# A spectral filter block on one core: the 2-D transform factored over the 128 row blocks first, then the columns, then one matrix per frequency group

## The chip, the core and the metric

The kernel runs on one core of one Trainium2 chip. The core has a matrix engine (TensorE, called PE in the profile; PEld is its weight load), a vector engine (DVE), a scalar engine (ACT), a general engine (POOL) and a synchronising engine (SP) that issues nearly all DMA transfers. The engines run their own instruction lists in order and meet at semaphores. PE writes only to PSUM, a small accumulation memory of eight banks; DVE and ACT copy results from there to SBUF. The metric is the device time of one execution in microseconds (us); lower is better.

## The reference, cut to what matters

```python
mod = (silu(c) @ w_mod)                   # -> sa, ca, ga, sb, cb, gb, each 640 wide
h = layernorm(x) * (1 + ca) + sa          # x: 2048 rows, 640 columns, bf16
X = rfft2(h, axes=(rows, columns))        # 2048 x 321 complex
y = irfft2(X * (w_r + 1j * w_i))          # the learned filter, 2048 x 321
x = x + ga * y
h = layernorm(x) * (1 + cb) + sb
x = x + gb * ((silu(h @ w_gate) * (h @ w_up)) @ w_down)     # 1728 hidden
```

## The kernel before

Row s of x is written s = 16p + t, with p = 0..127 on the partitions and t = 0..15 as 16 tiles of 128 rows by 640 columns. A row frequency k is written with 128 values k1 and 16 values k2. Column frequencies l and 320 - l are handled together: sums and differences of even and odd columns give both.

**Forward stage** (functions `ln1_*`, `turn`, `turned`, `dfwd`, `zcopy`, `s1`, `acopy`, in an order written out by hand in the string `plan`). For each tile t, DVE takes the statistics (L280, L283), ACT the square root (L251), DVE the reciprocal and the normalised tile `xn` (L293). PE turns it in five 128x128 transposes (L301), the turned tile is copied out, and six products of 328 columns against the table `Rs` (the column transform, with 1 + ca folded in) make `zps` (L309). After a copy (L318) eight products against `Gtab` (L332, L333) do the 128-point transform over p with the twiddle factors of t; the copy L343 stores `A_sb`.

**Middle stage** (`transposed`, `t2`, `stage_a`, `product`, `stage_b`, `evict_y`, `stage_c`). For 41 groups of four column frequencies, and their mirrored partners, blocks of `A_sb` are transposed, 64 of them by eight DMA transposes (L434), the rest on PE (L446). Two products with a 128x128 table do the 16-point transform over t (L463, L464), ACT copies `X` (L466), POOL adds the transform of sa in one row (L469), DVE multiplies by the filter (L479, two instructions for each `X`), PE turns back and adds the two halves of the complex product by multiplying with the identity (L488), the result is copied (L496, L498) and multiplied back over t (L512, L513) into `Ep` (L517, L519). The filter lies in `Wb` and in `Wq`, which is the mirrored half; `Wq` comes through a DRAM copy `Wneg` that reorders it (L217 to L223). One of its copies has its sign turned on DVE (L360).

**Inverse stage** (`s1inv`, `dinv`). For each t, ten products of 128 columns transform back over p (L673 to L679), ACT copies `VT` (L681, L682), six products of 320 columns transform back over d (L689), and DVE adds the result to x in two instructions (L692). The statistics of the second layer norm for the first four tiles are taken in between (L621 to L623), and `Rinv_sb` holds the inverse column table times ga.

**Feed-forward stage**: four blocks of 512 rows, each with 27 groups of five products of 512 columns (L727, L740), a Silu on ACT (L743), a product on DVE (L744), then 8 x 14 products of 320 columns (L774) and a store (L777).

SP issues transfers in program order, and the framework gives SP's transfers eight semaphores in turn, so that a transfer waits for the eighth one before it. PE, DVE, ACT and POOL also keep program order. PSUM tiles are shared by tag; a tag with one or two buffers makes the writer wait for the copy of an earlier tile.

Of the kernel before, what the change touches and what calls it, by code (L numbers as in the profile page):

```python
# [18 lines left out]
LH = 164  # L19
L = 2 * LH  # L20
NG = 41
LP = 2 * NG
LW = 324
# [12 lines left out]


_TABLE_CACHE = {}


def _tables():
# [3 lines left out]
    l = np.arange(161, dtype=np.float64)[None, :]  # L45
# [8 lines left out]
    p = np.arange(P, dtype=np.float64)[:, None]  # L54
    k1 = np.arange(128, dtype=np.float64)[None, :]
    G = np.zeros((P, NT, 3, 128))
    for t in range(NT):
        a = 2.0 * np.pi * ((k1 * (16 * p + t)) % S) / S
        G[:, t, 0, :] = np.cos(a)
        G[:, t, 1, :] = -np.sin(a)  # L60
        G[:, t, 2, :] = np.sin(a)
    T["G"] = G.astype(_NPBF)
    kk = np.arange(128, dtype=np.float64)[:, None]
    pp = np.arange(P, dtype=np.float64)[None, :]
    H = np.zeros((128, NT, 3, P))
    for t in range(NT):
        a = 2.0 * np.pi * ((kk * (16 * pp + t)) % S) / S
        H[:, t, 0, :] = np.cos(a)
        H[:, t, 1, :] = np.sin(a)
        H[:, t, 2, :] = -np.sin(a)  # L70
    T["H"] = H.astype(_NPBF)

    F16 = np.exp(-2j * np.pi * np.outer(np.arange(16), np.arange(16)) / 16)

    def fwd(F, turn):
        M = np.zeros((16, 2, 4, 2, 16, 4))
        for j in range(4):
            i = 3 - j if turn else j
            M[:, 0, j, 0, :, i] = F.real
            M[:, 1, j, 0, :, i] = -F.imag  # L80
            M[:, 0, j, 1, :, i] = F.imag
            M[:, 1, j, 1, :, i] = F.real
        return M.reshape(128, 128)


    def inv(F, turn):
        M = np.zeros((2, 16, 4, 16, 2, 4))
        for j in range(4):
            i = 3 - j if turn else j
            M[0, :, i, :, 0, j] = F.real  # L90
            M[1, :, i, :, 0, j] = -F.imag
            M[0, :, i, :, 1, j] = F.imag
            M[1, :, i, :, 1, j] = F.real
        return M.reshape(128, NT, 2, 4)

    G16 = np.exp(+2j * np.pi * np.outer(np.arange(16), np.arange(16)) / 16)
    K = np.zeros((128, 9, 128))
    K[:, 0, :] = fwd(F16, False)
    K[:, 1, :] = fwd(F16[:, ::-1], True)
    K[:, 2, :] = -K[:, 1, :]  # L100
    a, b = inv(G16, False), inv(G16[::-1], True).reshape(128, 128)
    K[:, 3, :] = K[:, 4, :] = a.reshape(128, 128)
    K[:, 5, :], K[:, 6, :] = b, -b

    K[:, 7, :] = np.stack([-a[:, :, 1], a[:, :, 0]], axis=2).reshape(128, 128)
    K[:, 8, :] = a.reshape(128, 128)
    T["K"] = K.astype(_NPBF)
# [4 lines left out]
    for odd in range(2):  # L112
        dd = 2 * h + odd

        def re_row(ll):
            return (1.0 if ll == 0 else 2.0) * np.cos(2.0 * np.pi * ((dd * ll) % D) / D) / (S * D)

        def im_row(ll):
            if ll == 160:
                w = -np.sin(0.5 * np.pi * dd) if odd else np.cos(0.5 * np.pi * dd)  # L120
                return 2.0 * w / (S * D)
            return -2.0 * np.sin(2.0 * np.pi * ((dd * ll) % D) / D) / (S * D)

        for r in range(128):
            Rinv[r, odd, 0] = re_row(r)
            Rinv[r, odd, 1] = im_row(r + 1)
        for r in range(32):
            Rinv[64 * odd + r, odd, 2] = re_row(128 + r)
            Rinv[64 * odd + 32 + r, odd, 2] = im_row(129 + r)
# [6 lines left out]
def adaln_block_kernel(  # L136
# [15 lines left out]
    G_dram = nc.inline_tensor(T["G"], name="tab_G").ap()  # L152
    H_dram = nc.inline_tensor(T["H"], name="tab_H").ap()
    K_dram = nc.inline_tensor(T["K"], name="tab_K").ap()
# [11 lines left out]
    Ktab = const.tile([P, 9, 128], BF16, name="Ktab")  # L166
# [3 lines left out]
    shat = const.tile([1, 2, 2, LH], F32, name="shat")  # L170
# [8 lines left out]
    identb = const.tile([P, 128], BF16, name="identb")  # L179
    sc_f = const.tile([P, NC5], F32, name="sc_f")  # L180
    sc_col = const.tile([P, NC5], BF16, name="sc_col")
    sa_col = const.tile([P, NC5], BF16, name="sa_col")
    sEO = const.tile([1, 2, 2, LH], F32, name="sEO")

    x_sb = big.tile([P, NT, D], BF16, name="x_sb", tag="b20")
    wm_ca = big.tile([P, NC5, D], BF16, name="wm_ca", tag="epx")
    wm_sa = big.tile([P, NC5, D], BF16, name="wm_sa", tag="b21b")
    wm_g = big.tile([P, NC5, 2 * D], BF16, name="wm_g", tag="wg")
    wm_sb = big.tile([P, NC5, D], BF16, name="wm_sb", tag="wu")
    Rinv_sb = big.tile([P, 2, 3, 320], BF16, name="Rinv_sb", tag="ri")  # L190
    Rp = big.tile([P, 6, L], BF16, name="Rp", tag="rp")
    Rs = big.tile([P, 6, L], BF16, name="Rs", tag="rs")
    Gtab = big.tile([P, NT, 3, 128], BF16, name="Gtab", tag="gt")
    Wb = big.tile([P, 3, NT, LH], BF16, name="Wb", tag="wb")
    Wq = big.tile([P, 3, NT, 160], BF16, name="Wq", tag="b35")
    Htab = big.tile([P, NT, 3, 128], BF16, name="Htab", tag="ht")

# [24 lines left out]
    for i in range(2):  # L222
        nc.sync.dma_start(Wq[:, i], Wneg[i])  # L223
# [47 lines left out]
    with tc.tile_pool(name="ph1", bufs=3) as ph1, \  # L271
# [39 lines left out]
        def dfwd(t):  # L311
            zs[t] = ps1.tile([P, 2, 512], F32, name="zps")
            for r in range(2):
                dmm(zs[t][:, r, :L], t, r)
# [511 lines left out]
```

## Time and profile before

| what | us |
|---|---|
| median of 3 runs | 280.5 (280.18 to 281.39) |
| the profiled execution, its own time | 280.83 |
| its span in the profile | 279.0 |
| forward stage, to the first transposing DMA | 0 to 37.7 |
| middle stage | 37.7 to 74.0 |
| inverse stage | 74.0 to 97.6 |
| feed-forward stage | 97.6 to 279.0 |

The span is what the instructions cover; 1.8 us of the execution lie outside it. A group line of the profile gives a kind of instruction, how many there were, their busy time and the mean duration of one. Instructions of one engine overlap a little, so a row of equal ones starts at shorter distances than a duration: five products of 128x512 last 379 ns each in the groups and take 1.08 us together.

### The profile page before, as it was taken

The page shows a single profiled execution, that of the slowest core. Times are in us where ns is not written, and L with a number is a line of the kernel's source. Part 1 is how long each engine was busy: PE and PEld are TensorE (multiplying, and loading weights), DVE is VectorE, ACT ScalarE, POOL GpSimd, SP SyncE. Part 2 cuts the span into 40 slices and gives each one's busy share as a digit, 9 for nine tenths or more (in the row PEclk, how much of TensorE's full clock was granted, in tenths as well). Part 3 has the DMA queues.
Part 4 walks back from the last instruction along what each step waited for, and adds up shares of the span by engine and source line. Part 5 has one row for each costly group of instructions (what it writes and reads, how often), then busy time and mean ns, then how long its engine had stood idle before and what let it go on. Part 6 is the DMA issues. An engine that isn't in the chain of part 4 may idle for free.

```text
span 279.0 us, 5262 instructions
## 1 busy us (share of the span) xinstructions
PE 268.6 (96%) x2120; PEld 170.3 (61%) x2120; DVE 163.6 (59%) x411; ACT 112.8 (40%) x220; POOL 10.5 (4%) x34
## 2 busy tenths in 40 slices
PE   6899979999899999999999999999999999999995
PEld 6567768998787844446754445764444774444673
DVE  4999966799499738876227845224872422422322
ACT  5998666998455663222022323003233103223000
POOL 1000023312000010000000000000000000000000
PEclk9999999999999999999999999999999999999999
DMA  7989999999994100050110050101013011000011
GB/s 263 411 220 209 349 324 183 220 307 366 356 363 77 29 27 6 0 96 0 49 56 3 0 96 0 47 26 33 0 33 63 25 47 35 1 0 2 0 47 47
DMA packets 40634, 30.82 MB, mean 110 GB/s; under 512 B 29281, under 2 KB 37410, under 8 KB 40482
## 3 DMA queue, kind: packets, MB, share of 16 engines
q1 hardware_dynamic: 40608, 30.49, 38.3%
q8 instruction: 16, 0.26, 0.4%
q14 instruction: 8, 0.07, 0.1%
q10 hardware_dynamic: 2, 0.00, 0.0%
HBM read 22.88 MB, written 3.93 MB: 96 GB/s over the span
## 4 chain that ended last, share of the span: by engine, by line
PE 74%; DMA 10%; SPq 9%; DVE 4%; ACT 1%; issue 1%; ACTq 0%; DVEq 0%
PE gps L740 20%; PE ups L740 20%; PE ob L774 11%; PE oa L774 10%; DMA Wd_sb<-in_B_w_down_dram 4%; SPq L218 4%; DMA wm_sa<-in_w_mod_dram 3%; DMA Gtab<-tab_G 2%; PE oa L689 2%; SPq L596 2%; PE gu L727 2%; PE ob L689 1%; DVE x_sb L692 1%; SPq L223 1%; PE yps L488 1%; PE xps L463 1%
## 5 line engine op out<-in xcount | busy, mean ns | idle before, releaser
L740 PE MATMUL gps<-h2T_all,Wg 128*128 128x512 bf16 x260 | 64.6, 379 | 0.0
L740 PE MATMUL ups<-h2T_all,Wu 128*128 128x512 bf16 x260 | 64.6, 379 | 0.0
L743 ACT ACTIVATE sg<-gps 128x512 f32<-128x512 f32 x52 | 31.0, 597 | 74.0 <-PE gps L740 72.3
L740 PEld LDWEIGHTS <-Wu 128*128 128x128 bf16 x260 | 25.5, 98 | 30.6
L740 PEld LDWEIGHTS <-Wg 128*128 128x128 bf16 x260 | 25.4, 98 | 30.5
L744 DVE TENSOR_TENSOR ATb<-ups,sg 128x512 bf16<-128x512 f32 x26 | 17.9, 690 | 32.0 <-PE ups L740 32.0
L744 DVE TENSOR_TENSOR ATa<-ups,sg 128x512 bf16<-128x512 f32 x26 | 17.9, 687 | 20.4 <-PE ups L740 17.5
L774 PEld LDWEIGHTS <-ATa 128*128 128x128 bf16 x224 | 21.9, 98 | 9.3 <-issue 0.5
L774 PEld LDWEIGHTS <-ATb 128*128 128x128 bf16 x224 | 21.9, 98 | 8.8
L730 ACT ACTIVATE sg<-gu 64x512 f32<-64x512 f32 x4 | 2.3, 586 | 46.6 <-PE gu L727 46.6
L776 DVE TENSOR_TENSOR xo<-ob,x_sb 128x320 bf16<-128x320 f32 x16 | 7.9, 492 | 22.1 <-PE ob L774 22.1
L776 DVE TENSOR_TENSOR xo<-oa,x_sb 128x320 bf16<-128x320 f32 x16 | 7.8, 491 | 18.4 <-PE oa L774 18.4
L774 PE MATMUL oa<-Wd_sb,ATa 128*128 128x320 bf16 x112 | 16.8, 299 | 0.1
L774 PE MATMUL oa<-Wd_sb,ATb 128*128 128x320 bf16 x112 | 16.5, 299 | 0.0
L774 PE MATMUL ob<-Wd_sb,ATb 128*128 128x320 bf16 x112 | 16.5, 299 | 0.0
L774 PE MATMUL ob<-Wd_sb,ATa 128*128 128x320 bf16 x112 | 16.5, 299 | 0.0
L309 PE MATMUL zps<-Rs,hT 128*128 128x328 bf16 x90 | 14.7, 303 | 0.1
L280 DVE BATCH_NORM_STATS2 st<-x_sb 128x6 f32<-128x320 bf16 x32 | 13.8, 470 | 0.8 <-DMA x_sb<-in_A_x_dram 0.8
L681 ACT CAST VT<-va 128x512 bf16<-128x512 f32 x16 | 9.4, 586 | 8.0 <-PE va L677 6.2
L488 PE MATMUL yps<-identb,PP 128*128 128x128 bf16 x162 | 11.5, 219 | 0.6 <-DVE PP L479 0.4
L466 ACT CAST X<-xps 128x512 bf16<-128x512 f32 (+1 forms) x21 | 11.2, 598 | 1.6 <-PE xps L464 1.6
L309 PEld LDWEIGHTS <-hT 128*128 128x128 bf16 x96 | 8.8, 98 | 4.8 <-ACT hT L305 0.8
(204 smaller groups left out, 407.0 us busy)
## 6 DMA issues: line engine op xcount, KB each, us to landing
out_dram<-xo SPq DMA_DIRECT2D x16, 160.0 KB, 1.8
Wg<-in_B_w_gate_dram SPq DMA_DIRECT2D x1, 2080.0 KB, 12.8
Wd_sb<-in_B_w_down_dram SPq DMA_DIRECT2D x1, 2080.0 KB, 13.4
Wu<-in_B_w_up_dram SPq DMA_DIRECT2D x1, 2080.0 KB, 9.7
x_sb<-in_A_x_dram SPq DMA_DIRECT2D x3, 640.0 KB, 9.3
wm_g<-in_w_mod_dram SPq DMA_DIRECT2D x2, 800.0 KB
Gtab<-tab_G SPq DMA_DIRECT2D x4, 384.0 KB, 8.2
Htab<-tab_H SPq DMA_DIRECT2D x1, 1536.0 KB, 7.1
```

The source lines that it names most:

```text
L218: nc.sync.dma_start(to[0:15, 0], wv[1:16, 0])
L280: nc.vector.bn_stats(sts[t][:, h, :], x_sb[:, t, 320 * h:320 * h + 320])
L309: nc.tensor.matmul(zap, lhsT=hTs[t][:, 2 * r + i, :], rhs=Rs[:, 3 * r + i, :], start=(i == 0), stop=(i == 2))
L466: nc.scalar.copy(X[:, :n].rearrange("p i c k j -> p i (c k j)"), xps[:, :n, :])
L488: nc.tensor.matmul(yps[:, i, :], lhsT=PP[:, i, cp].rearrange("p a k j -> p (a k j)"), rhs=identb[:], start=(cp == 0), stop=(cp == 1))
L681: nc.scalar.copy(VTs[t][:, 0:4, :], va[:])
L689: nc.tensor.matmul(os_[odd][:], lhsT=VT[:, 2 * odd + ci if ci < 2 else 4, :], rhs=Rinv_sb[:, odd, ci, :], start=(ci == 0), stop=(ci == 2))
L740: nc.tensor.matmul(o[:], lhsT=w_[:, c5, fc * 128:(fc + 1) * 128], rhs=h2T[:, :, c5, :], start=(c5 == 0), stop=(c5 == NC5 - 1))
L743: nc.scalar.activation(sg[:], gps[:], ACT.Silu)
L744: nc.vector.tensor_tensor(AT[:, fc, :], ups[:], sg[:], ALU.mult)
L774: nc.tensor.matmul(os_[h][:], lhsT=AT[:, fc, tok], rhs=Wd_sb[:, fc, h * 320:(h + 1) * 320], start=(fc == 0), stop=(fc == NFC - 1))
L776: nc.vector.tensor_tensor(xo[:, h * 320:(h + 1) * 320], os_[h][:], x1[:, t, h * 320:(h + 1) * 320], ALU.add)
```

## The change

The same function is computed with the three partial transforms in another order.

- **Over p first, without turning x.** A tile's five blocks of 128 columns are the stationary operand, and a real 128x128 table `Fs` (cosines and sines of the 128-point transform, times the row's 1/std) is the moving one, so one product transforms over p and turns at once (`turn`). The mean is taken off by four products with the negated mean, in a high and a low bf16 part made on POOL (`means`). There is no normalised tile and no twiddle table `Gtab`.
- **Then over d**, for 16 groups g of 8 rows of that result times 16 t: six products of 324 columns (`dfwd`), as before.
- **Then over t with a matrix for each group** (`over_t`), which holds the 16-point transform, the twiddles and the recombination of the real transform, and makes l and 320 - l side by side. The filter is multiplied on (`product`), the complex sums and the sums of the two halves are made on DVE (`sums`), and `over_t_back` multiplies by the group's inverse matrix.
- **Back over d, then over p** (`dinv`, `over_p`), with one addition to x for each tile.
- **The filter's layout.** `W` has on each partition one (half, b, k2) and 16 rows of the filter. It is loaded by 18 transfers in place of ten (with `Wneg`), 16 of them of some 160 KB to 16 partitions each and two of them parts of one such piece, with rows of 642 bytes. POOL then turns the upper half of each row round in place (`filter_part`, four parts), in front of the products of the four groups concerned.
- x is loaded first; `wm_ca` and `Rp` follow, then the filter with `wm_sa` and a quarter of the forward matrices `Mf` in the middle, then the rest of the tables. `Rs` and the product of `Rinv_sb` with ga move to POOL. In the feed-forward stage gate and up products share one two-bank PSUM tile with two buffers (`gu`, tag `vv`), where before they had two tags.

```diff
+    for a, b in ((0, 1), (1, 2), (2, 4), (4, 8), (8, 12), (12, 16)):
+        nc.sync.dma_start(x_sb[:, a:b, :], x_v[:, a:b, :])
     nc.sync.dma_start(wm_ca[:], wm_v[:, :, D:2 * D])
     nc.sync.dma_start(Rp[:], R_dram)
+    for i, w_ in enumerate((A_w_r, A_w_i)):
+        wv = w_.rearrange("(k2 r) l -> k2 r l", r=128)
+        for b in range(4):
+            nc.sync.dma_start(W[16 * b:16 * b + 16, :, i, 0:321], wv[:, 16 * b:16 * b + 16, :])
+            to = W[64 + 16 * b:80 + 16 * b, :, i, 0:321]
+            if b:
+                nc.sync.dma_start(to, wv[:, 128 - 16 * b:112 - 16 * b:-1, :])
+            else:
+                nc.sync.dma_start(to[:, 1:16], wv[:, 127:112:-1, :])
+                nc.sync.dma_start(to[:, 0], wv[:, 64, :])
+        if i == 0:
+            nc.sync.dma_start(wm_sa[:], wm_v[:, :, 0:D])
+            nc.sync.dma_start(Mf[:, 0:4], M_dram[:, 0:4])
+    nc.sync.dma_start(Mf[:, 4:8], M_dram[:, 4:8])
+    for j, i in enumerate((2, 4)):
+        nc.sync.dma_start(wm_g[:, :, D * j:D * (j + 1)], wm_v[:, :, D * i:D * (i + 1)])
+    nc.sync.dma_start(Mi[:, 0:8], Mi_dram[:, 0:8])
...
+        for q in range(9):
+            a, b = (2 * q, 2 * q + 2) if q < 7 else (7 + q, 8 + q)
+            for t in range(max(a, 1), b):
+                ln1_stats(t)
+            mh = means(a, b)
+            rstd_of(rstd1[:, a:b], mv1[:, a:b, 1])
+            nc.vector.reciprocal(rstd1[:, a:b], rstd1[:, a:b])
...
+        def filter_part(j):
+            g, gi = slice(4 * j, 4 * j + 4), slice(8 * j, 8 * j + 8)
+            tmp = ph2.tile([P, 4, 2, 160], BF16, name="wtmp", bufs=1)
+            tm1 = ph2.tile([P, 8, 2, 1], BF16, name="wtm1", bufs=1)
+            nc.gpsimd.tensor_copy(tmp[:], W[:, g, :, 320:160:-1])
+            nc.gpsimd.tensor_copy(W[:, g, :, LH:LH + 160], tmp[:])
+            nc.gpsimd.memset(W[:, g, :, 161:162], 0.0)
+            nc.gpsimd.tensor_copy(tm1[:], Wh[:, gi, :, 0:1])
+            nc.gpsimd.tensor_copy(Wh[:, gi, :, 0:1], Wh[:, gi, :, 128:129])
+            nc.gpsimd.tensor_copy(Wh[:, gi, :, 128:129], tm1[:])
...
+        def product(g, PP):
+            X = Xs.pop(g)
+            nc.vector.tensor_tensor(PP, X[:].unsqueeze(1).to_broadcast([P, 2, 2, L]),
+                                    W[:, g, :, :].unsqueeze(2).to_broadcast([P, 2, 2, L]), ALU.mult)
...
+        order = list(range(1, 11)) + [0] + list(range(11, 16))
+        units = [order[2 * u:2 * u + 2] for u in range(7)] + [order[14:15], order[15:16]]
...
+        LAG = 3
+        for n in range(NGR + LAG):
+            if n < NGR:
+                g = order[n]
+                over_t(g)
+                xcopy(g)
+                if g == todo[0][0]:
+                    PP = ph2.tile([P, 2, 2, 2, L], BF16, name="PP", bufs=2)
+                product(g, PP[:, todo[0].index(g)])
+                if g == todo[0][-1]:
+                    sums(todo.pop(0), PP)
+                if n + 2 < NGR:
+                    dfwd(order[n + 2])
+                    zcopy(order[n + 2])
+            if n >= LAG:
+                over_t_back(order[n - LAG])
+                vcopy(order[n - LAG])
+            if n == 2:
                 mod_cols(m_ps[:, 0], wm_g, 0)
...
+    def dinv(t):
+        o = ps3.tile([P, 2, 512], F32, name="oo", tag="oo")
+        for odd, blocks in enumerate(((0, 3, 4), (2, 1, 4))):
+            for i, b in enumerate(blocks):
+                nc.tensor.matmul(o[:, odd, 0:320], lhsT=V2[:, b, t, :, :].rearrange("p g j -> p (g j)"),
+                                 rhs=Rinv_sb[:, odd, i, :], start=(i == 0), stop=(i == 2))
+        W2s[t] = ph3.tile([P, 2, 320], BF16, name="W2")
+        nc.scalar.copy(W2s[t][:], o[:, :, 0:320])
+    def over_p(t):
+        W2 = W2s.pop(t)
+        y = ps3.tile([P, 2, 512], F32, name="yy", tag="vv")
         for odd in range(2):
+            nc.tensor.matmul(y[:, odd, 0:320], lhsT=Ftab[:, 1, :], rhs=W2[:, odd, :], start=True, stop=True)
+        nc.vector.tensor_tensor(x1v[:, t], y[:, :, 0:320], x1v[:, t], ALU.add)
```

One group g of the middle stage takes on PE: `dfwd`, 6 products of 324 columns; `over_t`, 4 of 324 and 8 of 162; `over_t_back`, 4 of 256 and 2 of 128. On ACT it takes three copies from PSUM, of 648, 648 and 640 columns. `sums` takes for a pair of groups two DVE instructions of 648 elements, two of 512 and eight of 62 to 66; the last two groups are taken singly. `zps` has two PSUM buffers, `xps` and `vps` one each, `X` two buffers in SBUF.

## The prediction

> **What bounds the kernel now.** I read the busy shares first, then the chain that ended last, then the busy time by stage, then the groups and short stretches of the timeline. The page's first part and the engine shares of the chain:
>
> ```profile
> PE 268.6 (96%) x2120; PEld 170.3 (61%) x2120; DVE 163.6 (59%) x411; ACT 112.8 (40%) x220; POOL 10.5 (4%) x34
> ...
> PE 74%; DMA 10%; SPq 9%; DVE 4%; ACT 1%; issue 1%; ACTq 0%; DVEq 0%
> ```
>
> PE is the bound as a whole. The stretches of the four stages (us, then busy us of PE, PEld, DVE, ACT, POOL, clock, DMA share, GB/s) show where that leaves room:
>
> ```profile
> 0.00:37.70 37.70, 33.90 (x320) 24.32 (x321) 31.55 (x98) 29.64 (x54) 0.71 (x6) 1.00 0.95 297
> 37.70:74.00 36.30, 33.60 (x536) 30.43 (x534) 28.45 (x67) 28.03 (x61) 8.85 (x26) 1.00 1.08 285
> 74.00:97.60 23.60, 23.10 (x282) 19.02 (x282) 19.41 (x51) 13.38 (x35) 0.00 (x0) 1.00 0.57 174
> 97.60:279.00 181.40, 178.04 (x991) 96.52 (x987) 84.19 (x197) 41.73 (x70) 0.98 (x2) 1.00 0.11 28
> ```
>
> The last stage, 181.4 us, is PE alone and keeps its instructions. The change is decided in the first 97.6 us, where transfers run nearly all the time (DMA share 0.95 and 1.08). So I ask when the feed-forward stage starts; now that is 97.6.
>
> **The durations.** Engine groups, and how DVE's statistics and ACT's root follow one another:
>
> ```profile
> L280 DVE BATCH_NORM_STATS2 st<-x_sb 128x6 f32<-128x320 bf16 x32 | 13.8, 470 | 0.8 <-DMA x_sb<-in_A_x_dram 0.8
> L309 PE MATMUL zps<-Rs,hT 128*128 128x328 bf16 x90 | 14.7, 303 | 0.1
> L318 ACT CAST Z<-zps 128x656 bf16<-128x656 f32 x13 | 9.2, 708 | 0.7 <-PE zps L309 0.2
> ...
> 3.83 0.89 DVE L280 BATCH_NORM_STATS2 st<-x_sb 128x6 f32<-128x320 bf16 x2 [0.78 <-DMA x_sb<-in_A_x_dram]
> 4.75 0.21 DVE L283 BATCH_NORM_AGGREGATE mv<-st 128x2 f32<-128x12 f32 x1
> 4.88 0.44 DVE L280 BATCH_NORM_STATS2 st<-x_sb 128x6 f32<-128x320 bf16 x1
> 5.33 0.16 DVE L289 RECIPROCAL rstd<-rstd 128x1 f32<-128x1 f32 x1
> ```
>
> A tile's statistics take 4.88 - 3.83 = 1.05 us of DVE; if DVE then waits for the root, the reciprocal is over at 5.49, 0.6 later, say 0.65.
>
> **Forward stage.** Five transposes, a normalised tile and eight `Gtab` products a tile go; on PE there come some 0.8 us a tile. DVE now has only statistics, but waits for ACT's root in every step q: seven pairs of 2 x 1.05 + 0.65 = 2.75, two singles of 1.70, together 22.65, so from 3.83 to 26.5. POOL's `means` run during that wait. Then a chain with nothing beside it: scaling 0.3, `turn` 1.0, DVE's copy of 640 columns 0.8, `dfwd` 1.0, ACT's copy 0.7, `over_t` 1.3, ACT's copy 0.7: the first filter product can start at 32.3.
>
> **The filter's arrival.** POOL's part 0 needs all 18 transfers of `W`, behind x, `wm_ca` and `Rp`. How fast transfers go, how long a piece takes that is as large as one of `W`, and POOL beside DVE:
>
> ```profile
> 8.00:12.00 4.00, 3.47 (x35) 2.25 (x33) 3.75 (x15) 3.63 (x9) 0.00 (x0) 1.00 1.03 412
> ...
> out_dram<-xo SPq DMA_DIRECT2D x16, 160.0 KB, 1.8
> ...
> 44.61 1.40 POOL L541 TENSOR_TENSOR shat<-sEO 1x256 f32<-1x256 f32 x2 [0.50 <-ACT sEO L539]
> ...
> 45.43 1.21 DVE L479 TENSOR_TENSOR PP<-X,Wq 128x512 bf16<-128x512 bf16 x2
> ```
>
> By the one-microsecond stretches before this one, 3.9 MB had moved by 12.1; x, `wm_ca` and `Rp` are 2.62 + 0.82 + 0.50 = 3.94 MB. Then 2.63 MB of `W`. No transfer of before goes to 16 partitions only, so I bound it. Best: 412 GB/s like the others, 6.4 us. Worst: 412 GB/s over 128 partitions is 3.2 GB/s for one, 51 GB/s for 16, 51 us. Nearest: the store of 160 KB, 1.8 us each, of which the issue (0.33) overlaps with the piece before: 16 x 1.47 = 23.5 us. I take it, since a piece that feeds few partitions can't be expected to overlap with the next as a full one does. `wm_sa` and `Mf`'s first quarter, 1.34 MB, lie between (3.3 us), and the last landing costs 1.0: `W` is complete at 12.1 + 23.5 + 3.3 + 1.0 = 39.9.
>
> The Trainium skill, page "SBUF — State Buffer", section "Door 1: The DMA port swizzle", says that partitions 0 to 15 reach four of 16 ports, with 104 GB/s measured at 1 MiB. By the skill's page `W` takes an estimated 25.3 us and the forecast would be 1.8 us later, 293.1; no run here shows it yet.
>
> **POOL in front of the product.** A part is two copies of 1280 elements, a small memset, three copies of 16. POOL's memsets of 640 and 512 columns take 626 and 519 ns (0.84 ns an element), its sums of 256 and 72 floats 719 and 492 at most (1.23 ns): 1.2 to 2.0 us a copy. I take 1.3, since a copy reads one input; with 0.24 for each small one (L469) and hand-overs, 3.6 us a part (3.3 to 4.9). The first product starts at 39.9 + 3.6 + 0.2 = 43.7, 11.4 after the 32.3. `wm_g` (at 45) and `Mi` (at 48) come behind `W` and meet PE after the first pair's sums: no further wait.
>
> **Middle stage.** PE: 328 columns start each 0.137 apart, so a group costs 0.82 + (0.55 + 0.56) + 0.55 = 2.47 us. ACT: three copies at 0.6, 1.8 us. DVE: `PP` of 512 elements starts each 0.335 apart, 0.27 for two elements a cycle and 0.07 fixed; so 0.75 for a product of 1296, 0.41 for 648, 0.335 for 512, 0.14 for a small one: a pair 1.5 + 0.82 + 0.67 + 1.12 + hand-overs 0.1 = 4.2, a single 2.65, together 7 x 4.2 + 2 x 2.65 = 34.7 us. At one element a cycle the large product would add 16 x 0.67 = 10.8; the rows of `PP` speak for two.
>
> POOL's parts 1 to 3 and the two products for `Rinv_sb` (1.6 each) are 14.0 us that run beside DVE's two-input products. Of the two `PP` shown, which take 0.74 elsewhere, one lasted 868 ns instead of 412 while POOL's 719 ns sum ran, 0.456 more: 0.63 of POOL's time. Bounds: 0 and all 14.0; I take 0.63 x 14.0 = 8.9. The last result needs `over_t_back` and its copy, 1.5. From 43.7: 34.7 + 8.9 + 1.5 = 45.1, to 88.8.
>
> The Trainium skill, same page, section "SBUF: two separate sides", has POOL and a two-input DVE instruction exclude one another for whole instructions. By the skill's rule all 14.0 would be paid, an estimated 5.1 us more; the shown row agrees that one is held up, with less than the whole.
>
> **Inverse stage.** Before, PE was the limit: 23.6. Now PE has 8 x 0.137 = 1.09 a tile, 17.4. DVE: 16 additions of 640 floats from PSUM at 0.71 (L692: 0.36 for 320), 11.4; four statistics, 4.2; four normalised tiles 1.5, reciprocal 0.2, three scalings 1.05: 18.3. With the first tile's way through PE and ACT (2.0), less the last addition (0.7), for which the feed-forward stage's first tile does not wait, 19.6. DVE is the limit, 4.0 shorter than before. `Wd_sb` and `Wu` (4.3 MB, 10.4 us at 412 GB/s) hide under it; without that cover they would cost their excess.
>
> **Feed-forward stage.** A gate product now waits for the DVE product two steps back, not for ACT's Silu; DVE ends 0.7 after the up product and the tile is wanted 2.16 after it. I cost it at nothing; the cover is that 1.4 us, and DVE's folds and layer norm in the first block come to 14 of 17 us, lagging by up to 0.9.
>
> **Sum.** Start of the feed-forward stage 88.8 + 19.6 = 108.4 against 97.6: +10.8. The profiled execution took 280.83, 0.33 over the median of 280.5, and would come to 291.6; on the median 291.3.
>
> **Rivals.** (1) *The pieces land like other loads.* For it: transfers over all partitions ran at 412 GB/s. Against: each piece goes to an eighth of the partitions. `W` is there at 22.8, POOL's part 0 ends at 30.1, inside DVE's statistics, and the middle stage runs at PE's pace: from 30.3, 16 x 2.47 + 0.8 for sa + 5.4 for the last group's way through ACT, DVE and PE = 46.5, to 76.8, + 19.6 = 96.4, -1.2, or 279.3; with the first x tile half as large, landing 0.5 to 1 us sooner, 278.5. It decides when a piece takes under 0.76 us ((28.5 - 12.1 - 3.3 - 1.0) / 16), and while POOL costs DVE less than its slack of 16 x 2.47 - 34.7 = 4.8 us. (2) *The pieces land fast but POOL stops DVE.* Parts 1 to 3 and `Rinv_sb` then fall on DVE from 32.3: 11.8 x 0.63 = 7.4 less some 2 of slack: +5.4 on rival 1, 284. (3) *The pieces go at one partition's rate.* `W` at 67.4, 27.5 later: 319. A slot of POOL's upper prices (4.9 a part, all of 14.0 on DVE) with the forecast's arrival gives 291.3 + 1.3 + 5.1 = 298.
>
> **How the numbers follow.** Forecast 0.61, with its own range of 286 to 303 by 5.1 less or more for POOL, copies, and pieces between 1.2 and 1.8 us; rival 1 0.15, rival 2 0.19, rival 3 0.05. Leaving out 1 and 3 (0.20) gives 281 to 303. About 0.5%, 1.4 us, is what a measurement here can tell: faster 0.15 from rival 1, same 0.05 from rival 2's lower end, the rest slower.
>
> **What would show it.** Right: the chain passes through transfers of `W` and POOL's copies; DVE idles 10 us before its first product waiting for POOL; the inverse stage lasts near 20. Wrong: `W` complete before 28 us, no long waits of DVE for POOL, or an unchanged-looking feed-forward stage that is longer than 181.4.

## The result, and the profile after

The changed kernel takes 313.85 us (median of 4 runs, 313.29 to 316.67) against 280.34 for the kernel before: 1.121 times as long (95% interval 1.113 to 1.128), 33.5 us where 10.8 were forecast. It lies outside the forecast range of 281 to 303. The profiled execution took 313.29, with a span of 311.5. Times of the variants below are medians of all their runs; by the fast runs alone `e1_adds_after` is 298.8, `e7_warm` 292.7 (one run) and `e14_together` 297.6 us (the profiles of the first and the last are of their slowest run), and no conclusion hangs on the difference.

Busy shares of the engines and engine shares of the chain that ended last, changed kernel:

```profile
PE 273.1 (88%) x1839; PEld 162.8 (52%) x1839; DVE 163.9 (53%) x416; ACT 107.8 (35%) x189; POOL 34.9 (11%) x70
...
PE 65%; DVE 16%; DMA 13%; issue 3%; ACT 2%; SPq 1%; DVEq 0%
```

PE's work has hardly grown (268.6 before), but its share has fallen from 96% to 88%, and DVE's share of the chain has gone from 4% to 16%. The stretches of the stages, cut at the first filter product, the first `dinv` product and the first feed-forward product (columns as before: length, busy us of PE, PEld, DVE, ACT and POOL, clock, DMA share, GB/s):

```profile
0.00:42.70 42.70, 28.44 (x270) 20.36 (x271) 18.32 (x62) 23.22 (x51) 16.55 (x48) 0.92 1.01 243
42.70:93.38 50.68, 43.72 (x455) 33.28 (x454) 43.21 (x124) 30.73 (x51) 18.39 (x23) 0.93 0.59 209
93.38:115.67 22.29, 19.85 (x128) 12.89 (x129) 17.67 (x34) 12.08 (x19) 0.00 (x0) 0.93 0.28 75
115.67:311.50 195.83, 181.15 (x990) 96.31 (x987) 84.70 (x198) 41.76 (x69) 0.00 (x0) 1.00 0.10 26
```

| stage, by the forecast's terms | forecast | measured | difference |
|---|---|---|---|
| first filter product starts | 43.7 | 42.7 | -1.0 |
| from there to `dinv` | 45.1 | 50.7 | +5.6 |
| inverse stage | 19.6 | 22.3 | +2.7 |
| feed-forward stage | 181.4 | 195.8 | +14.4 |
| span | 289.8 | 311.5 | +21.7 |

Two thirds of the error is in the stage that was costed at nothing. PE's waits from 115.67 on (releaser, us in total, times, longest), then a stretch of PE's and of DVE's timeline at the end of the first block:

```profile
PE oo L652 <- DVE xo L654: 10.4, 16, 1.1
PE yy L576 <- ACT W L570: 0.8, 1, 0.8
PE gu L621 <- DVE ATa L625: 0.4, 1, 0.4
PE oo L652 <- DVE Wd_sb L631: 0.3, 1, 0.3
```

```profile
149.70 3.96 PE L652 MATMUL oo<-Wd_sb,ATa 128*128 128x320 bf16 x28 [1.07 <-DVE xo L654]
154.25 3.96 PE L652 MATMUL oo<-Wd_sb,ATa 128*128 128x320 bf16 x28 [0.58 <-DVE xo L654]
...
149.17 0.48 DVE L654 TENSOR_TENSOR xo<-oo,x_sb 128x320 bf16<-128x320 f32 x1
151.80 0.49 DVE L654 TENSOR_TENSOR xo<-oo,x_sb 128x320 bf16<-128x320 f32 x1 [2.15 <-PE oo L652]
153.70 0.49 DVE L654 TENSOR_TENSOR xo<-oo,x_sb 128x320 bf16<-128x320 f32 x1 [1.41 <-PE oo L652]
```

PE works in runs of 28 products and then stands, sixteen times, once for each row tile; it goes on when DVE's addition that started at 153.70 is over. Before, the two halves `oa` and `ob` were two tiles, and their products had next to no idle time before them (the last column):

```profile
L774 PE MATMUL oa<-Wd_sb,ATa 128*128 128x320 bf16 x112 | 16.8, 299 | 0.1
L774 PE MATMUL ob<-Wd_sb,ATa 128*128 128x320 bf16 x112 | 16.5, 299 | 0.0
```

Now they are halves of one tile `oo`, and the addition of the first half (L654) is issued between the products of the two halves, so that the second half's products wait for it. The list of changes ahead of the prediction names the shared gate/up tile, but not this one.

The first product comes late because POOL's part 0 waits for `W`. But `X`, the product's other input, is ready less than 1 us sooner, at 41.75:

```profile
39.19 1.25 POOL L354 COPY wtmp<-W 128x1280 bf16<-128x1280 bf16 x1 [5.33 <-DMA W<-in_A_w_i_dram]
41.05 0.70 ACT L401 CAST X<-xps 128x648 bf16<-128x648 f32 x1 [0.54 <-PE xps L396]
```

### The profile page after: what moved, and what is told of

Read it like the earlier page. It is cut to its first block, busy times and chain, and to the rows that moved or that the text cites. A ratio compares the mean times of both kernels' runs of the same rounds, so it can differ in the third digit from the quotient of the medians.

```text
span 311.5 us, 4641 instructions
## 1 busy us (share of the span) xinstructions
PE 273.1 (88%) x1839; PEld 162.8 (52%) x1839; DVE 163.9 (53%) x416; ACT 107.8 (35%) x189; POOL 34.9 (11%) x70
## 4 chain that ended last, share of the span: by engine, by line
PE 65%; DVE 16%; DMA 13%; issue 3%; ACT 2%; SPq 1%; DVEq 0%
PE gu L621 35%; PE oo L652 19%; DMA wm_ca<-in_w_mod_dram 4%; DMA W<-in_A_w_i_dram 4%; DVE xo L654 3%; DMA W<-in_A_w_r_dram 3%; DMA wm_g<-in_w_mod_dram 3%; DVE x_sb L577 3%; DVE PP L406 2%; PE oo L567 2%; PE zps L367 2%; DVE S L420 2%; PE xps L396 2%; PE xps L391 1%; PE gu L608 1%
## 5 line engine op out<-in xcount | busy, mean ns | idle before, releaser
L624 ACT ACTIVATE sg<-gu 128x512 f32<-128x512 f32 x52 | 31.1, 598 | 79.2 <-PE gu L621 74.5
L654 DVE TENSOR_TENSOR xo<-oo,x_sb 128x320 bf16<-128x320 f32 x32 | 15.7, 491 | 51.9 <-PE oo L652 51.9
L652 PE MATMUL oo<-Wd_sb,ATa 128*128 128x320 bf16 x224 | 32.5, 299 | 6.0 <-DVE xo L654 5.4
L652 PE MATMUL oo<-Wd_sb,ATb 128*128 128x320 bf16 x224 | 32.0, 299 | 4.9 <-DVE xo L654 4.9
L625 DVE TENSOR_TENSOR ATb<-gu,sg 128x512 bf16<-128x512 f32 x26 | 17.9, 689 | 33.3 <-ACT sg L624 33.2
L621 PE MATMUL gu<-h2Ta,Wg 128*128 128x512 bf16 x130 | 32.3, 379 | 0.4 <-DVE ATa L625 0.4
L621 PE MATMUL gu<-h2Ta,Wu 128*128 128x512 bf16 x130 | 32.3, 379 | 0.0
L621 PE MATMUL gu<-h2Tb,Wu 128*128 128x512 bf16 x130 | 32.3, 379 | 0.0
L621 PE MATMUL gu<-h2Tb,Wg 128*128 128x512 bf16 x130 | 32.3, 379 | 0.0
L625 DVE TENSOR_TENSOR ATa<-gu,sg 128x512 bf16<-128x512 f32 x26 | 17.8, 686 | 21.6 <-ACT sg L624 21.5
L567 PE MATMUL oo<-Rinv_sb,V 128*128 128x320 bf16 x96 | 17.1, 321 | 0.8 <-ACT V L446 0.8
```

What stands on the lines that cost most here:

```text
L567: nc.tensor.matmul(o[:, odd, 0:320], lhsT=V2[:, b, t, :, :].rearrange("p g j -> p (g j)"), rhs=Rinv_sb[:, odd, i, :], start=(i == 0), stop ...
L621: nc.tensor.matmul(o, lhsT=w_[:, c5, fc * 128:(fc + 1) * 128], rhs=h2T[:, :, c5, :], start=(c5 == 0), stop=(c5 == NC5 - 1))
L624: nc.scalar.activation(sg[:], gps, ACT.Silu)
L625: nc.vector.tensor_tensor(AT[:, fc, :], ups, sg[:], ALU.mult)
L652: nc.tensor.matmul(oo[:, h, 0:320], lhsT=AT[:, fc, tok], rhs=Wd_sb[:, fc, h * 320:(h + 1) * 320], start=(fc == 0), stop=(fc == NFC - 1))
L654: nc.vector.tensor_tensor(xo[:, h * 320:(h + 1) * 320], oo[:, h, 0:320], x1[:, t, h * 320:(h + 1) * 320], ALU.add)
```

## The experiments

Runs with the changed kernel's 18 transfers of `W` scatter by 1 to 3% (313.3 to 316.7 in that kernel, 297.1 to 303.5 in `e1_adds_after`, 292.7 to 301.8 in `e7_warm`), and so does the time at which `W` is complete: POOL's part 0 started at 35.8, 39.2, 41.9 and 45.1 in four kernels. So stages are compared by their profiles, and times only where they differ by more.

### One tile for two halves

`e1_adds_after`, the changed kernel with

```diff
                 for fc in range(NFC):
                     nc.tensor.matmul(oo[:, h, 0:320], ...)
-                nc.vector.tensor_tensor(xo[:, h * 320:(h + 1) * 320], oo[:, h, 0:320], ...)
+            for h in range(2):
+                nc.vector.tensor_tensor(xo[:, h * 320:(h + 1) * 320], oo[:, h, 0:320], ...)
```

> The changed kernel with both halves of `oo` multiplied before the first of the two additions (L654) is issued. Theory A (the two halves share one PSUM tile, so the second half's matmuls wait for DVE's addition of the first): the 16 waits of `oo` for `xo`, 10.4 us in the trace, and what the interrupted stream costs beside them go; the feed-forward stage returns from 195.8 to 182 to 184 us and the time falls by 12 to 14 us, to 300 to 302. Theory B (the stage is longer because gate and up share one tile, or because PE starts it at a worse clock): the waits of `oo` move but the time stays within 2 us of 313.9.

`e2_before_shared`, the kernel before with

```diff
-            os_ = [ps3.tile([P, 320], F32, name=n) for n in ("oa", "ob")]
+            oo = ps3.tile([P, 2, 512], F32, name="oo", tag="oo")
```

> The kernel before with its two accumulators `oa` and `ob` made halves of one two-bank tile `oo`, the additions where they are. Theory A: the feed-forward stage grows by 16 x 0.74 = 11.9 us or a little more, the time from 280.3 to 292 to 295, and PE shows some 16 waits of `oo` for `xo` of 0.6 us. Theory B: within 2 us of 280.3.

Measured: 299.7 us (297.1 to 303.5) and 294.9 us (293.8 to 295.9; the kernel before beside it 281.3, ratio 1.046, 1.040 to 1.052). PE's waits in the feed-forward stage, first of `e1_adds_after`, then of `e2_before_shared`:

```profile
PE yy L576 <- ACT W L570: 0.8, 1, 0.8
PE gu L621 <- DVE ATa L625: 0.4, 1, 0.4
PE oo L652 <- DVE Wd_sb L631: 0.3, 1, 0.3
```

```profile
PE oo L774 <- DVE xo L776: 9.8, 16, 1.1
```

The sixteen waits go where the additions come last and appear where the tile is shared. From its first product to the end the stage lasts 181.5 us before, 193.9 in `e2_before_shared`, 195.8 in the changed kernel and 183.3 in `e1_adds_after`: 12.4 us for the shared tile in the one, 12.5 in the other. `e2_before_shared` also starts the stage 2.7 us later (100.2 against 97.5); its `dinv` writes the same tile, but that part was not followed up. Theory A holds; of the single gate/up tile only one wait of 0.4 us is to be seen.

### Why the filter comes late

Six layouts of the same 2.6 MB. `e3_w_wide` and `e12_w_rows` keep 16 transfers of 256 rows, `e15_one_piece` has one per input; in these three the rows go to other places than their frequencies, so the filter is another one:

```diff
-        wv = w_.rearrange("(k2 r) l -> k2 r l", r=128)
+        wv = w_.rearrange("(g p) l -> p g l", p=128)   # e3_w_wide
+        wv = w_.rearrange("(p g) l -> p g l", p=128)   # e12_w_rows, e15_one_piece
...
+        for b in range(8):                             # e3_w_wide, e12_w_rows
+            nc.sync.dma_start(W[:, 2 * b:2 * b + 2, i, 0:321], wv[:, 2 * b:2 * b + 2, :])
+        nc.sync.dma_start(W[:, :, i, 0:321], wv)       # e15_one_piece
```

> The changed kernel with the same bytes of `W` in rows of the same 642 bytes and in 16 transfers of 256 rows as before, but each transfer spread over all 128 partitions instead of 16. The order of the filter's rows is then not that of the frequencies, so the filter itself is another one. Theory C (pieces are slow because each feeds 16 partitions): `W` is complete at 23 to 27 us instead of 39.2, POOL's part 0 then follows POOL's `means` at 33 to 35, the first product starts at 36.5 to 39 and the time falls by 3.5 to 6 us. Theory D (the rows of 642 bytes or the number of transfers set the pace): part 0 still starts at 38 to 40 and the time stays within 1 us.

> The changed kernel with `W` in 16 transfers of 256 rows over all 128 partitions, as in the run with wide pieces (345 GB/s), but each partition's 16 rows lie one behind the other in the source (a partition reads 10 KB on end, its neighbour the next 10 KB), as a partition's rows do in the changed kernel; the filter is then another one. Theory C3 (what counts is how many partitions a transfer fills: 16 or 64 run at 160 to 200, 128 at 345): 330 to 390 GB/s from 12 to 28, part 0 without a wait for `W` at 30 to 33, time 304 to 307. Theory D2 (what counts is the order in which the source is read): 160 to 200 GB/s, part 0 waits and starts at 35 to 45, time 308 to 316.

> The changed kernel with `W` in one transfer per input over all 128 partitions, 16 rows of 642 bytes for each partition (the filter is then another one). Sixteen partitions, 64 neighbours and 64 interleaved ones, each with 16 rows for a partition in a transfer, ran at 150 to 200 GB/s; 128 partitions with 2 rows ran at 345. Theory C6 (what slows a transfer is many rows one behind the other into the same partition): 160 to 200 GB/s, part 0 of POOL waits for `W` until 33 to 38, 308 to 316 us. Theory C7 (what counts is that a transfer fills all 128 partitions): 330 to 390 GB/s, part 0 at 30 to 33 without a wait, 304 to 308 us.

`e5_strided` keeps 16 partitions a piece but takes every fourth; `e8_wide` (with the additions last) has 64 neighbouring partitions in a transfer, `e13_all_ways` 64 interleaved ones. Columns and rows of `M` and `Mi` follow in each:

```diff
-            nc.sync.dma_start(W[16 * b:16 * b + 16, :, i, 0:321], wv[:, 16 * b:16 * b + 16, :])
+            nc.sync.dma_start(W[b:64:4, :, i, 0:321], ...)       # e5_strided
+        nc.sync.dma_start(W[0:64, :, i, 0:321], wv[:, 1:65, :]...)    # e8_wide
+        nc.sync.dma_start(W[0:128:2, :, i, 0:321], wv[:, 1:65, :]...) # e13_all_ways
```

> The changed kernel with the filter's frequencies in another order over the partitions: each transfer of `W` still has 160 KB in rows of 642 bytes for 16 partitions, but every fourth one (0, 4, 8, ...) instead of 16 neighbours; the columns and rows of the two tables `M` and `Mi` follow. Theory C1 (what is slow is 16 neighbouring partitions, which share few ways into the memory): the transfers run at 330 to 400 GB/s as with all 128 partitions, POOL's part 0 starts when its last `means` is over (30 to 33), the first product at 38.5 to 40 and the time falls by 7 to 9 us, as in the run with wide pieces. Theory C2 (16 partitions are few wherever they lie): 150 to 200 GB/s as now, and no change within 1 us.

> The changed kernel with both additions after both halves of `oo`, and the filter's frequencies ordered so that one transfer of 0.66 MB fills 64 partitions (two for each of the two inputs, and a row of 10 KB for group 0 later). Theory C (few neighbouring partitions make the pieces slow): 330 to 400 GB/s from 12 to 28, `W` complete by 28, POOL's part 0 without a wait for a transfer behind its last `means`; the first product is then 7.4 to 9 us behind the last reciprocal (31.6 to 33.2 in the runs in which `W` was early), at 39 to 42, and the time 290 to 294, with less scatter than 297 to 303.5. If 64 partitions are as slow as 16, 298 to 303.

> As the kernel with one transfer per half of the frequencies and input (64 partitions, 0.66 MB, 163 GB/s and part 0 at 35.8), but with the two halves interleaved: the lower frequencies on the even partitions, the upper ones on the odd, so that each transfer still fills 64 partitions, spread over all 128; the tables `M` and `Mi` follow. Theory C4 (a transfer runs at the rate of the ways into the memory that its partitions reach, and 64 neighbours reach half or less): 330 to 390 GB/s between 12 and 28, `W` complete before the last `means`, POOL's part 0 without a wait at 30 to 33, the time 290 to 295. Theory C5 (64 partitions are too few wherever they lie, or rows read in the wrong order are): 160 to 200 GB/s, part 0 at 35 to 40, 296 to 300.

Stretches of four us with `W` in flight, of the changed kernel, `e3_w_wide`, `e15_one_piece` and `e13_all_ways` in this order:

```profile
16.00:20.00 4.00, 2.05 (x22) 1.36 (x19) 2.87 (x10) 3.06 (x9) 1.76 (x2) 0.77 1.18 174
28.00:32.00 4.00, 3.28 (x34) 2.35 (x33) 1.33 (x6) 2.94 (x7) 0.61 (x3) 0.95 1.15 155
```

```profile
16.00:20.00 4.00, 3.36 (x18) 1.97 (x17) 3.34 (x12) 2.73 (x6) 4.00 (x5) 0.57 1.09 352
```

```profile
16.00:20.00 4.00, 2.06 (x27) 1.44 (x25) 2.69 (x10) 2.89 (x9) 3.23 (x4) 0.50 1.08 334
```

```profile
16.00:20.00 4.00, 1.26 (x28) 0.88 (x27) 1.72 (x6) 1.91 (x6) 0.76 (x1) 0.50 1.17 176
```

In the last two columns the DMA engines are busy all the time in each (a share over 1), but they move 155 to 176 GB/s where a transfer has 16 or 64 partitions and 334 to 352 where it has all 128. `e12_w_rows` ran at 329 to 347 from 12 to 24, `e8_wide` at 163 and 166 in the two stretches shown first. Among the layouts to all 128 partitions neither the rows per partition in a transfer (2 or 16), nor its size (160 KB to 1.3 MB), nor the order in the source matters. That half of the rows are read backwards is not what holds the others back: in `e11_two_queues`, below, two transfers to 64 partitions that are read forwards ran at 147 from 16 to 20. One difference is left that no run separates from the number of partitions: in all layouts below 200 GB/s, and in `e5_strided`, a transfer's source jumps by 128 rows from one k2 to the next, and in those above 300 its partitions lie 1 or 16 rows apart. `e5_strided` lay between (193 to 274 in its stretches with pieces of `W`), and part 0 waited 0.45 us there. The Trainium skill, page "SBUF — State Buffer", section "Door 1: The DMA port swizzle", counts the ports that the partitions reach; by that rule interleaved partitions would have been fast, and 173 to 188 GB/s in stretches of four us in `e13_all_ways` and `e14_together` speak against it as the whole cause. The page "DMA: Bandwidth & Descriptors", section "The descriptor swizzle", says that a transfer to 128 partitions is split so that each engine writes one port; the fast layouts are just those. How the others are split no run here shows.

Times: `e3_w_wide` 305.7, `e12_w_rows` 307.2, `e15_one_piece` 308.5, `e5_strided` 307.5 (against 313.85), `e8_wide` 297.5 and `e13_all_ways` 300.0 (against 299.7). In the last two part 0 still waited, until 35.8 and 37.5. An early filter is worth 5 to 8 us and no more, and most of it not by an earlier first product (1.8 us in `e12_w_rows`): the middle stage lasts 45.7 us there for 50.7. Three of POOL's four parts are over there when the first product starts; how much of the 50.7 is the changed kernel's own is told further down. POOL's part 0 and DVE in `e12_w_rows`:

```profile
30.24 1.25 POOL L348 COPY wtmp<-W 128x1280 bf16<-128x1280 bf16 x1
...
31.73 0.16 DVE L311 RECIPROCAL rstd<-rstd 128x1 f32<-128x1 f32 x1 [2.30 <-ACT rstd L238]
33.73 0.82 DVE L293 CAST hT<-tp 128x640 bf16<-128x640 f32 x1 [1.83 <-PE tp L289]
40.88 1.36 DVE L400 TENSOR_TENSOR PP<-X,W 128x1296 bf16<-128x1296 bf16 x1 [6.33 <-ACT X L395]
```

Part 0 starts without a wait. The last reciprocal waits 2.30 us for a root that stands on ACT behind `sa_cols`, which waits for PE; and from it to `X` there are 9.1 us instead of the 6.4 of the changed kernel, since PE's clock is at half and the twelve `dfwd` products take 3.40 us instead of 1.82. The first product waits for `X` now, and comes at 40.88 instead of 42.70.

### POOL beside DVE

`e4b_no_filter` leaves the mirror copies out:

```diff
-        for j in range(4):
-            filter_part(j)
-    nc.gpsimd.memset(W[:, :, :, L - 2:L], 0.0)
+    nc.gpsimd.memset(W[:, :, :, L - 3:L], 0.0)
```

> The changed kernel without POOL's copies that mirror and swap the filter's columns (`filter_part`), so the filter's second half and two columns are left as loaded or zero. Theory E (POOL's copies hold DVE's two-input instructions up): the first product starts at about 39.3 instead of 42.7, the long `PP`, `S` and `Ex` of the first two pairs (3.59, 2.88, 1.27, 2.62 us) fall to 1.5, 0.8, 0.2, 1.5, the first 6 us of hold-up go, only the 3.45 us beside `Rinv_sb`'s products stay, and the time falls by 6 to 9.5 us. Theory F (the middle stage is set by PE's pace anyway): the time falls by the 3.5 us of the earlier start alone.

Measured 340.3 us: a miss of another kind. The memset now begins right behind the last column that `W`'s transfers write; it starts only at 38.83, by the profile behind a transfer, and every `means` of POOL stands behind it. The forward stage cannot be used, the middle stage can: 46.2 us from the first product (72.40) to `dinv` (118.57), with DVE busy for 36.4. A cleaner pair is `e9_forward` and `e10_dve`, below, of which the second has two of the four parts and `Rinv_sb`'s products on DVE. DVE's groups `PP` and `S` of the changed kernel, then of `e10_dve`:

```profile
L406 DVE TENSOR_TENSOR PP<-X,W 128x1296 bf16<-128x1296 bf16 x16 | 16.0, 1017 | 8.7 <-DMA wm_g<-in_w_mod_dram 4.9 <-ACT X L401 3.8
...
L420 DVE TENSOR_TENSOR S<-Y 128x512 bf16<-128x512 bf16 (+1 forms) x18 | 11.9, 701 | 0.8
```

```profile
L409 DVE TENSOR_TENSOR PP<-X,W 128x1296 bf16<-128x1296 bf16 x16 | 13.1, 831 | 4.7 <-ACT X L404 4.7
...
L423 DVE TENSOR_TENSOR S<-Y 128x512 bf16<-128x512 bf16 (+1 forms) x18 | 6.4, 393 | 0.9
```

DVE is busy for 43.21 us of the middle stage in the changed kernel and for 35.96 in `e10_dve`, of which 2.3 are `Rinv_sb`'s products: 33.7 us of its own, so 9.5 us of hold-up. (`e11_two_queues`, below, with all copies on DVE, gives 33.5.) It is seen at its plainest here, one engine's line after the other's, in the changed kernel:

```profile
59.48 4.25 POOL L483 TENSOR_TENSOR Rinv_sb<-Rinv_sb,ga_bc 128x960 bf16<-128x960 bf16 x2 [3.75 <-DMA ga_bc<-ga_row]
...
59.80 4.21 DVE L420 TENSOR_TENSOR S<-Y 128x512 bf16<-128x512 bf16 x2
```

Two sums that take 0.76 us elsewhere take 4.21. Holding up works both ways and reaches copies too: POOL's copies of 1280 elements last 1.25 us alone and up to 1.84 beside DVE; DVE's last 0.50 alone (`e11_two_queues`) and up to 1.56 beside POOL (`e10_dve`).

### The half clock

`e7_warm` (with the additions last):

```diff
+            if n >= NGR - 1:
+                keep_warm(ps1, "zps", 2, 12)
```

> The changed kernel with both additions after both halves of `oo`, and 12 products of an identity put on PE after each of the last four groups' copies at the end of the middle stage, where PE otherwise waits 0.8 us at a time. If the half clock of 90 to 96 comes of these waits, the clock is granted in full from 89 to 97, the first twelve products of `dinv` take 1.8 us instead of 3.4, and the inverse stage falls by 1 to 2 us (22.3 to 20.5); the time by as much. If the clock falls for another reason (the work before, a budget), 0.50 stays and the time rises by up to 1 us.

Stretches of 2 us around the end of the middle stage in the changed kernel (the clock is the third number from the end), and on PE's timeline the first `dinv` products of the changed kernel and of `e7_warm`:

```profile
88.00:90.00 2.00, 1.68 (x50) 1.45 (x47) 1.86 (x7) 1.10 (x4) 0.52 (x1) 0.97 1.11 364
90.00:92.00 2.00, 1.22 (x8) 0.80 (x7) 0.79 (x9) 0.69 (x1) 0.00 (x0) 0.50 1.02 340
92.00:94.00 2.00, 1.22 (x7) 0.65 (x6) 0.00 (x0) 0.69 (x1) 0.52 (x1) 0.50 1.02 396
94.00:96.00 2.00, 2.00 (x9) 1.10 (x8) 0.00 (x0) 0.67 (x1) 0.00 (x0) 0.50 0.77 297
```

```profile
93.38 3.38 PE L567 MATMUL oo<-Rinv_sb,V 128*128 128x320 bf16 x12 [0.78 <-ACT V L446]
```

```profile
86.65 1.80 PE L569 MATMUL oo<-Rinv_sb,V 128*128 128x320 bf16 x12
```

With the identity products the granted clock stays at 1.00 from 81 to 91, the twelve products take 1.80 us instead of 3.38, and the inverse stage 20.95 instead of 22.3. The time, 299.5 (292.7 to 301.8), is lost in the scatter of `W`, so that only the stage shows it.

### All of it mended

`e6_pipe`, `e9_forward`, `e10_dve`, `e11_two_queues` and `e14_together` put several edits together, all with the additions last. The main ones:

```diff
+            for t in range(b, min(b + (2 if q < 6 else 1), NT)):   # ahead of the reciprocal
+                ln1_stats(t)
-            if q == 3:
-                for i in range(6):
+            if 3 <= q < 6:
+                for i in range(2 * q - 6, 2 * q - 4):              # Rs, two in a step
...
+            e = (nc.gpsimd, nc.vector, nc.vector, nc.gpsimd)[j]    # filter_part, e10_dve
...
+                nc.scalar.dma_start(W[64:128, :, q, 0:321], ...)   # e11_two_queues, at q = 0 and 1
```

> The changed kernel with both additions after both halves of `oo`, the statistics of the next tiles put on DVE ahead of the reciprocal of these ones, and POOL's six products for `Rs` spread over three steps, two in each. Against that kernel without the two other edits (299.7): if the first product waits for POOL's part 0 and that for `W` alone, part 0 still starts at 38 to 40 and the time stays within 1.5 us, although the statistics end some 5 to 8 us earlier. If the statistics and POOL's `means` carry a part of it (W's issues can't be held up by them), the first product comes earlier by that part, and the time falls by up to 3 us.

> The kernel with wide pieces, and in the forward stage the next tiles' statistics ahead of the reciprocal of these ones, POOL's products for `Rs` two in a step, `mpsB` and its copy moved behind the first group of the middle stage, and products of an identity on PE where it waits before the first `dfwd` and at the end of the middle stage. If the chain of roots, reciprocals and `means` is what is left in the forward stage: the last reciprocal at 24 to 27, the first product at 31 to 35, and the time 281 to 287. If the first product then waits for `W` or for POOL's part 0 (behind `means` and `Rs`), it stays at 36 to 40 and the time at 287 to 292.

> As the kernel before it, with parts 1 and 2 of the filter's mirror copies on DVE, and the two products for `Rinv_sb` on DVE beside the tenth and twelfth group. If POOL holding DVE up costs time in the middle stage: that stage (46 to 47 us in these runs from the first product to `dinv`) falls to 44 to 45.5, and the time by 1 to 3 us against the kernel with POOL doing both. If PE's pace hides it, the two are within 1 us; if DVE's copies run at one element a cycle and lie in front of the first product, slower by up to 2 us.

> All edits together: additions after both halves; one transfer per half of the partitions and input, the lower half's on SP's queue and the upper half's on ACT's, ahead of `wm_sa` and `Mf`; statistics ahead of reciprocals; `Rs` in three steps; `mpsB` behind the first group; products of an identity in PE's waits; all four parts of the filter's copies on DVE, three of them in its waits of the forward stage; `Rinv_sb`'s products on DVE; the gates' columns (`m_ps`) two groups later. If the two halves of the partitions are filled at once at 330 GB/s or more: `W` complete at 22 to 26, first product at 33 to 37, 44 us of middle stage, 20.5 of inverse, 182.5 of feed-forward: 281 to 288. If 64 partitions at a time stay slow, DVE's copies wait for `W` ahead of the last reciprocals: first product at 40 to 45, 288 to 294. It is ahead of the kernel before (281.3) only if the first product starts before 33.

> All that helped, together: additions after both halves of `oo`; interleaved halves of `W` ahead of `wm_sa` and `Mf`; statistics ahead of reciprocals; `Rs` in three steps; `mpsB` behind the first group; products of an identity in PE's waits; the filter's copies and `Rinv_sb`'s products on DVE, none on POOL; `m_ps` two groups later. If `W` is complete at 21 to 24 (theory C4): last reciprocal at 28 to 30, first product at 35 to 37, `dinv` at 81 to 84 with 46 to 48 us of PE-bound middle stage, 20.5 of inverse stage, feed-forward from 102 to 105: 285 to 289, still over the 281.3 of the kernel before. With `W` at 28 to 36 (theory C5) DVE's copies wait in front of the last reciprocals: 290 to 297.

| run | time, us | last reciprocal | first product | `dinv` | feed-forward starts |
|---|---|---|---|---|---|
| `e6_pipe` | 299.9 | 32.59 | 45.40 | 92.69 | 115.14 |
| `e9_forward` | 294.5 | 28.30 | 39.56 | 87.81 | 108.75 |
| `e10_dve` | 293.8 | 30.57 | 43.79 | 87.72 | 108.66 |

- `e6_pipe`: as foreseen, the statistics end early and nothing comes of it; part 0 waits 12.67 us for `W`, until 41.9.
- `e9_forward`: the last reciprocal is early, but part 0 waits 8.94 us for `W`, until 36.07. The first product at 39.56 is the expectation's second case, since the pieces of 64 partitions are slow; the time is 2.5 us over that case's.
- `e10_dve`: DVE's copies delay the first product by 4.2 us and the middle stage is 4.3 shorter, so that `dinv` starts when it did in `e9_forward`; the time differs by 0.7 us, less than two runs of `e9_forward` do (293.8 and 295.3). What the copies no longer hold up they cost in front, or PE sets the pace in both: these two runs don't tell which.
- `e11_two_queues`, 319.5 us: a miss. The first of ACT's two transfers went out only at 30.48, when a small transfer of SP's to the same tile (10 KB, issued at 20.29) had landed 10.1 us after its issue, and all that ACT had queued stood behind it for 22.2 us:

```profile
ACT rstd L245 <- DMA W<-in_A_w_r_dram: 22.2, 1, 22.2
```

Its middle stage, which had nothing of POOL's beside it but 1.67 us, lasted 48.2 us with PE busy for 46.02, some 3 of them for identity products: there PE is busy all but 2 us.
- `e14_together`, 298.5 us (295.3 to 301.3): theory C5's case and worse, `W` at 34.9 with DVE's copies standing in front of the last two reciprocals.

None of them beats the kernel before (281 to 283 beside them). The best, `e10_dve`, is 1.041 times as long (1.032 to 1.049): 11 us of its loss lie before the feed-forward stage (108.66 against 97.5).

## Why the prediction was right in sign and wrong in size

**The step that failed: "I cost it at nothing", of the feed-forward stage.** The prediction looked at the gate/up tile alone, with a cover of 1.4 us, and that cost 0.4. The same edit made the down stage's two accumulators one tile, with an addition between its halves, and that was not followed: 12.5 us by two runs from both sides. The prediction's own rows had the greater part of the price, an addition of 320 columns (0.36 us there, 0.49 here). With the hand-overs it makes sixteen waits of PE of 0.58 to 1.07 us, and what the interrupted runs cost beside them. The rest of the stage's 14.4 are the wait for the last `W2` (0.8), two single waits (0.4 and 0.3), and some 0.4 not followed up.

**The filter's arrival and POOL's part in front: right, with luck, and with an error hidden behind it.** Part 0 started at 39.2 for 39.9 forecast, and took 3.5 us for 3.6. By the Trainium skill's page "SBUF — State Buffer", section "Door 1: The DMA port swizzle", the estimate was 41.7. Other runs of the same transfers had it from 35.8 to 45.1, so the agreement to 0.7 is luck; the range given for a piece, 1.2 to 1.8 us, means 35.6 to 45.2 and held. But "the first filter product can start at 32.3" was wrong: `X` was ready at 41.75. The last reciprocal came at 35.3 for 26.5, because DVE waited for ACT's roots up to 4.82 us at a time; these stood behind copies that waited for PE, which waited for POOL's six `Rs` products (6.5 us), and at the end behind `sa_cols`, which waited for `mpsB`. The chain from there to `X` took 6.4 us for 5.8. All this hid behind `W` and part 0 by less than 1 us. So rival 1 (279.3) had no chance here: with `W` early, `e3_w_wide` still took 305.7, some 293 without the shared tile's 12.5. (Its sum does not come out either: 16 x 2.47 + 0.8 + 5.4 is 45.7, not 46.5.)

**The hold-up of DVE by POOL: right in size.** 8.9 us were forecast and 9.5 measured, about half of the 18.4 us for which POOL was busy in that stage; DVE's own work was 33.7 measured, 34.7 forecast. But little of it reached the time, as the next point shows.

**The middle stage, 50.7 for 45.1: the model was too simple.** It took DVE for the only limit. But the stage lasted 45.7 to 46.2 us also where DVE was busy for only 36.4 to 37.3 (`e12_w_rows`, `e15_one_piece`, `e4b_no_filter`), and 47.3 in `e1_adds_after` and `e6_pipe`, which have the changed kernel's code in this stage and its hold-up (DVE busy for 43.1). So some 6 us of hold-up make 1 to 2 us of stage. PE is as close a limit: it is busy for 39.6 to 43.7 us in these runs, since the gates' columns, their transpositions and `sa` come to the sixteen groups, and in `e11_two_queues`, with POOL out of the way, the stage took 48.2 with 46.0 of PE (its identity products included). The changed kernel's 3.4 us over `e1_adds_after` are its own: the two sums above made PE wait for 1.76 us, and then twelve products ran at half clock (66 to 69), which cost an estimated 1.6 (3.3 us for 1.65 in `e1_adds_after`). That the stage was forecast within 2.2 us of these 47.3 is luck.

**The inverse stage, 22.3 for 19.6:** 1.3 of the 2.7 us are the half clock (20.95 in `e7_warm`); the remainder wasn't tested.

**Against the rivals.** Rival 2 (284) had the hold-up but an early filter; rival 3 (319, one partition's rate for a piece) was not what happened, though its time is nearest. The prediction had named "an unchanged-looking feed-forward stage that is longer than 181.4" as what would make it wrong, and gave it no chance.

## What to carry to other kernels

When two accumulators become halves of one tile, ask who reads the first half while the second is being written, at every place that uses the tile, not only at the one the edit is about; move the read behind both, or keep two tiles. A stage that "keeps its instructions" is costed at nothing only after its waits were gone through tile by tile. And a transfer's price depends on its form: look for a row of a transfer of the same form before costing it; here those to all 128 partitions moved twice as much in the same time. Last, a hold-up of one engine is not yet time: ask which other engine would set the pace without it.

## What the runs showed of the hardware that was not expected

- DMA engines that are busy all the time moved 147 to 188 GB/s (in stretches of four us) with 16 neighbouring partitions or 64, neighbouring or interleaved, in a transfer, and 329 to 358 with all 128. The sources of the former also have jumps of 128 rows, which no run took out.
- PE's granted clock fell to 0.50 for some 3.4 us after a wait of 1.76 us and a shorter one, and for some 6.4 through a chain of waits of 0.8 us. The Trainium skill, page "TensorE: Matmul & The Clock Gate", section "Why this matters for your kernels", asks for no gaps over some 3 us; here shorter ones were enough. But the length alone does not decide: waits of 1.32 and 1.01 us ahead of the first `dfwd` products left the clock at 1.00 in the changed kernel (34 to 44), and the same two were followed by 0.50 in `e12_w_rows` (33 to 39).
- POOL's and DVE's copies and two-input sums lengthen each other: 0.76 us to 4.21, 0.50 to 1.56, 1.25 to 1.84.
